# Attention and two gated layers on one core: the planner's order replaced by a written sequence, and the last block's end by product pairs

## The chip, the cores and the metric

The kernel runs on 1 core of a Trainium2 chip. The metric is device time in microseconds (us), the median of a few runs. TensorE (PE) multiplies, VectorE (DVE), ScalarE (ACT) and GpSimd (POOL) work element by element, and SyncE (SP) issues nearly all DMAs. Each engine works through its own queue in order.

## The reference

```python
def _attn_ref(q, k, v, tau):                    # batch 4, heads 8, sequence 576, head size 64
    scores = np.matmul(q, k.transpose(0, 1, 3, 2)) / np.sqrt(64)
    thresh = np.max(scores, axis=-1, keepdims=True) - tau
    scores = np.where(scores >= thresh, scores, -1e9)
    attn = np.exp(scores - np.max(scores, axis=-1, keepdims=True))
    attn = attn / (np.sum(attn, axis=-1, keepdims=True) + 1e-09)
    return np.matmul(attn, v)

x = attn_out.transpose(0, 2, 1, 3).reshape(2304, 512)
h = x @ w_in                                     # 512 x 2048
x = (h * np.tanh(softplus(h))) @ w_out           # 2048 x 512
h = x @ w2_in                                    # 512 x 2048
out = (h * np.clip(h + 3.0, 0.0, 6.0) / 6.0) @ w2_out
```

## The kernel before

**Attention.** The queries of a batch are cut into five tiles of 128 rows (the fifth, the tail, has 64), and two heads go together: 16 head pairs, 80 tiles. Pairs run batch by batch. One tile is a chain of steps: the scores `s` on PE (L1845), their row maximum `pk` on DVE (L1854), the exponentials `ex` on ACT (L1864) with the threshold `th` (L1859), the mask `mk` on DVE (L1867, it reads the scores and writes e_ex), the f16 half `ph` on ACT (L1872) and the rest `pl` on POOL (L730), a DMA transpose `tr` issued by SP (L1880), the product with v, `pv`, on PE (L1893), the division on DVE (L1963 to L1970), a transpose on PE (L2007) and x in two f16 halves. A score tile occupies its PSUM bank until the mask has read it. Loads of attention are `lq` (q, L1760), `lk` (k, L1757; ACT scales k, L1765) and `lv` (v, L1727, with maxima `vm` on DVE, L1709).

**Weights.** The four matrices come as words of 64 bits, in pieces of 1 MB (`lr`, L872). A piece is read by DVE for its top (L786), converted on ACT, POOL and DVE (L938 reads the raw buffer last) and split in f16 halves. There are two raw buffers.

**Layers.** The 2304 tokens are nine blocks of 256: blocks 0 to 7 are two full query tiles of one batch each, block 8 is the four tails. The first product of the first layer (`g`, L1237) of blocks 0 to 5 is worked off in small pieces beside attention. The second product (`y`, L1352) follows. The second layer (L1377 onward) computes both its products from quarters, with seven products in place of eight. For a block there are two units of first-half products (`g0a` to `g1g`, L1426), sums on DVE (L1454, L1519, L1082, L730) and ACT (L1513), the gated halves `oh` on ACT (L1529) and `o` on DVE (L730), then eight feature steps `y` (L1579) of 21 matmuls each, 3 for each of the seven products 0 to 6. The seven sums lie in PSUM, two to a bank. From them the result is put together: ACT takes product 0 as the seed `v` (L1619), DVE adds the others (`va` to `vg`, L1623), and SP stores (L1636).

**What sets the order.** Each step is a task with the engines that may do it, a cost, what it depends on and the buffers it needs. Class `Plan` (L511) keeps a clock for each engine and picks the task that can start next, by priorities, offsets and a table of some thousand corrections (`NUDGE`). Instructions are issued in the order in which tasks are picked. Which buffer of a ring a task takes follows from the order too.

**The last block.** In block 8 the last two feature steps are done pair by pair, in the order `ORDER_OUT`: products 0 and 5, then 6 and 4, then 2 and 3, then 1. The first four lie in one tile of two banks (ring `r_y`, called y_y), the same ring that block 7's sums use, the others in two tiles of one bank each (ring `r_h`). Each quarter of the result is stored by two DMAs of 64 x 256, all on SP's queue, since the tail rows of a pair of batches go to two places.

Of the kernel before, what the change touches and what calls it, by code (L numbers as in the profile page):

```python
# [21 lines left out]
P = 128  # L22
# [15 lines left out]
COL = 4  # L38
ORDER = (0, 0, 0, 0, 1, 0, 0, 1, 1, 1, 1)
LAST = (1, 1)  # L40
ORDER_OUT = (0, 5, 6, 4, 2, 3, 1)
# [3 lines left out]
WARM_WINDOW = 3.413  # L45
RELEASE = dict.fromkeys(("s", "m", "h", "y", "aux"), 0.27)

STEP = 2.791
START = 12
PV_OFF = 3.422  # L50
V_FIRST = -0.435
FIRST_AHEAD = 3
PREP_AHEAD = 5.76
CONV_STEP = 1
CONV_AT = 5.423
LATE_STEP = 3.76
# [24 lines left out]
LAG = 4
# [2141 lines left out]
```

## Time and profile before

| | |
|---|---|
| median of 3 runs | 978.81 us (976.41 to 979.07) |
| span of the profiled execution | 977.3 us |
| PE busy | 923.8 us, 95% |
| DVE busy | 766.2 us, 78% |
| ACT busy | 649.9 us, 66% |
| POOL busy | 401.6 us, 41% |

The profile is one execution, taken by the hardware. Its own time is the span, and the runs' median stands 1.5 us above it. Rows of the timeline give a start, a duration, the engine, the line, the operation, what is written from what, how many instructions are merged in the row, and in brackets the idle time of that engine before it with the instruction that ended it.

### The profile page before, as it was taken

What the parts mean: (1) busy time and instruction counts of PE and PEld (TensorE: products, weight loads), DVE (VectorE), ACT (ScalarE), POOL (GpSimd) and SP (SyncE); (2) the same over time, 40 slices, a digit from 0 to 9 for tenths busy, and PEclk for the clock granted to TensorE, in tenths of its full rate; (3) what the DMA queues carried; (4) which work ended last, traced back from release to release, by engine and by line L of the source; (5) the groups of instructions that cost most, each with busy time, mean ns of one, the idle gap of its engine ahead of it and who ended that gap; (6) DMA issues with size and microseconds to landing.
All of it is one profiled execution on the core that took longest, in us unless ns stands there. A gap on an engine that the chain in (4) does not pass through costs nothing.

```text
span 977.3 us, 25801 instructions
## 1 busy us (share of the span) xinstructions
PE 923.8 (95%) x10776; PEld 799.4 (82%) x10776; DVE 766.2 (78%) x1432; ACT 649.9 (66%) x1051; POOL 401.6 (41%) x354
## 2 busy tenths in 40 slices
PE   3679789999999999999999999999999999999996
PEld 1457467777777778888888888999999999999986
DVE  6987698888888887369999889787767757758864
ACT  6778688888888877567876778565354444444541
POOL 2777676766655666225656777710000000000000
PEclk9759789999999999999999999999999999999999
DMA  9899999999999999864665757760210210110001
GB/s 313 192 238 229 252 227 214 235 258 220 229 224 274 212 218 244 236 245 174 238 218 196 276 185 270 249 223 2 60 61 2 60 57 6 61 40 23 23 17 29
DMA packets 201796, 164.46 MB, mean 168 GB/s; under 512 B 174160, under 2 KB 174928, under 8 KB 195280
## 3 DMA queue, kind: packets, MB, share of 16 engines
q1 hardware_dynamic: 201680, 162.82, 62.0%
q8 instruction: 85, 1.39, 0.6%
q14 instruction: 31, 0.25, 0.1%
HBM read 84.28 MB, written 36.04 MB: 123 GB/s over the span
## 4 chain that ended last, share of the span: by engine, by line
PE 81%; DVE 10%; DMA 5%; ACT 1%; issue 1%; SPq 1%; POOL 1%; DVEq 0%; ACTq 0%; POOLq 0%
PE y_y L1352 16%; PE h_g L1237 16%; PE s_s L1845 8%; PE aux_pv L1893 6%; PE hp_g1a L1426 5%; PE h_g0a L1426 5%; PE hp_g1d L1426 2%; PE h_g0d L1426 2%; DMA raw_lr<-in_moe_w_in 2%; DVE e_ex L1867 2%; DVE nm_pk L1854 1%; DMA pt_tr<-p_ph 1%; PE h_g1b L1426 1%; PE hp_g0b L1426 1%; DVE top L786 1%; PE y_y__1_8_0_14998 L1579 1%
## 5 line engine op out<-in xcount | busy, mean ns | idle before, releaser
L730 POOL TENSOR_TENSOR p_ph<-e_ex,p_ph 128x128 f16<-128x128 f32 (+3 forms) x160 | 185.8, 1184 | 110.7 <-issue 54.8
L1579 PEld LDWEIGHTS <-gs_h 128*128 128x128 f16 x1512 | 146.8, 98 | 18.0 <-issue 1.5
L1426 PEld LDWEIGHTS <-w__h 128*128 128x128 f16 x2016 | 156.0, 98 | 0.6
L1854 DVE TENSOR_REDUCE nm_pk<-s_s 128x1 f32<-128x576 f32 x144 | 104.6, 751 | 31.1 <-PE s_s L1845 30.1
L1867 DVE SCALAR_TENSOR_TENSOR e_ex<-s_s,thr_th,e_ex 128x576 f32<-128x576 f32 x144 | 111.8, 811 | 17.8 <-ACT thr_th L1859 13.2
L1864 ACT ACTIVATE e_ex<-s_s,nm_pk 128x576 f32<-128x576 f32 x144 | 104.1, 730 | 17.0 <-DVE nm_pk L1854 14.2
L1845 PE MATMUL s_s<-kd_lk,qs_qp 64*128 64x288 f32 x440 | 81.7, 487 | 34.0 <-DVE e_ex L1867 25.4
L1872 ACT ACTIVATE p_ph<-e_ex 128x576 f16<-128x576 f32 x144 | 94.8, 679 | 12.5 <-DVE e_ex L1867 8.7
L1426 PEld LDWEIGHTS <-w__u 128*128 128x128 f16 x1008 | 98.6, 98 | 0.0
L1893 PEld LDWEIGHTS <-pt_tr 128*128 128x128 f16 x2016 | 81.8, 103 | 9.9 <-issue 5.8
L1845 PEld LDWEIGHTS s_s<-kd_lk,qs_qp 64*128 64x128 f32 x440 | 42.6, 209 | 55.2 <-issue 35.9
L1893 PE MATMUL aux_pv<-vh,pt_tr 128*128 128x65 f16 (+1 forms) x1296 | 86.6, 204 | 0.8 <-DMA pt_tr<-p_ph 0.8
L730 DVE TENSOR_TENSOR gs_h<-g_ab,gs_h 128x896 f16<-128x896 f32 x72 | 74.6, 1086 | 15.9 <-ACT gs_h L1529 15.9
L1529 ACT ACTIVATE gs_h<-g_ab 128x1792 f16<-128x1792 f32 x36 | 59.6, 1690 | 27.4 <-DVE g_ab L730 27.4
L1893 PE MATMUL aux_pv<-vl_vl,pt_tr 128*128 128x64 f16 x720 | 70.9, 203 | 0.0
L1513 ACT ACTIVATE g_ab<-g_ab,aux,hscales 128x512 f32<-128x512 f32 x72 | 54.1, 805 | 16.9 <-DVE g_ab L1454 16.9
L1286 ACT ACTIVATE he_t<-h_g,hin 128x512 f32<-128x512 f32 x63 | 42.9, 683 | 22.4 <-PE h_g L1237 18.3
L1323 ACT ACTIVATE hp_e<-hl_l 128x512 f32<-128x512 f32 x72 | 42.4, 595 | 21.7 <-DVE gs_h L1332 21.3
L1519 DVE SCALAR_TENSOR_TENSOR g_ab<-g_ab,f 128x512 f32<-128x512 f32 x72 | 51.2, 746 | 5.0 <-ACT g_ab L1513 5.0
L1332 DVE SCALAR_TENSOR_TENSOR gs_h<-hp_e,fscales,gs_h 128x512 f16<-128x512 f32 x72 | 52.9, 742 | 1.9 <-ACT gs_h L1326 1.8
L1326 ACT ACTIVATE gs_h<-hp_e,fscales 128x512 f16<-128x512 f32 x72 | 47.4, 680 | 9.5 <-PE y_y L1352 8.9
L1444 ACT ACTIVATE s_ka<-h_g0a 128x512 f32<-128x512 f32 x27 | 16.1, 595 | 48.4 <-PE h_g0a L1426 48.2
(651 smaller groups left out, 2523.3 us busy)
## 6 DMA issues: line engine op xcount, KB each, us to landing
hd<-he_t SPq DMA_DIRECT2D x36, 512.0 KB, 3.7
hl_l<-hd SPq DMA_DIRECT2D x18, 1024.0 KB, 5.6
raw_lr<-in_moe_w_in SPq DMA_DIRECT2D x16, 1024.0 KB, 5.8
raw_lr<-in_moe_w_out SPq DMA_DIRECT2D x16, 1024.0 KB, 7.4
yd<-yl_zhy SPq DMA_DIRECT2D x9, 896.0 KB, 3.8
qs_qp<-in_q SPq DMA_DIRECT2D x10, 576.0 KB, 6.0
v_lv<-in_v SPq DMA_DIRECT2D x16, 320.0 KB, 4.8
kd_lk<-in_k SPq DMA_DIRECT2D x15, 288.0 KB, 4.2
```

The costliest lines, as they stand in the source:

```text
L730: engine[e].tensor_tensor(dst, a, b, ALU.subtract)
L1237: mm(hv[:, j, :], wj[:, wl, c * P : (c + 1) * P], x.tile[:, c, xl, :], start=j == 0 and n == 0, stop=j == 1 and n == 11, skip_group_check= ...
L1352: mm(yv[:, h, :], wt[1][f // 2].tile[:, f % 2, wl, c * P : (c + 1) * P], gs[fp // COL].tile[:, fp % COL, gl, f % 2, :], start=fp == 0 and ...
L1426: mm(dst.tile[:, i * Q : (i + 1) * Q], wt[2][fp][wl].tile[:, right - 1, c * P : (c + 1) * P], x[xl].tile[:, c, left - 1], start=first and ...
L1529: nc.scalar.activation(part.tile[:, :, 0], g.tile[:, :, 1:], AF.Copy)
L1579: mm(region(p), part[:, gl, left - 1], wt[3][fp][wl].tile[:, right - 1], start=fp == n == 0 and spot(p)[1] == 0, stop=fp == NG - 1 and n == 2,
L1845: mm(s[j].tile[:, half, :HALF], lh[r], rh[r], start=m == 0, stop=m == len(terms) - 1,)
L1854: nc.vector.tensor_reduce(neg.tile[:, j : j + 1], sv(j), AX.XY, ALU.max, negate=True)
L1864: nc.scalar.activation(ev(j), sv(j), AF.Exp, bias=neg.tile[:, j : j + 1])
L1867: nc.vector.scalar_tensor_tensor(ev(j), sv(j), thr.tile[:, j : j + 1], ev(j), ALU.is_ge, ALU.mult)
L1872: nc.scalar.activation(p16.tile[:, js, :S], e_.tile[:, js], AF.Copy)
L1893: mm(ov[:, dst, :d], pt.tile[:, j, ch, :], part.tile[:, src, vc, :], start=i == j == ch == 0 and part is vh, stop=j == w - 1 and ch == 8, ...
```

## The change

The planner's cost model is removed: its constants, `NUDGE`, costs and priorities of all tasks, and the clocks. `Plan.run` now takes the next name from a string of 4094 tokens, each a step and its engine, and issues it. The tasks are the same but for the last block's end, and each runs on the engine that it had, but for one store. The sequence differs from the planner's order locally; on PE it is nearly the same, and the number of PE's instructions is equal.

```diff
-ORDER_OUT = (0, 5, 6, 4, 2, 3, 1)
+ENDS = ((0, 1), (5, 6), (4, 2), (3,))
+END_FPS = 3
...
     def run(self, until=None):
-        while self.left and (until is None or any(t.end is None for t in until)):
-            best = None
-            for e in self.clock:
-                c = self._candidate(e)
...
+        while self.tasks if until is None else not all(t.done for t in until):
+            name, _, e = next(self.sequence).partition("@")
+            task = self.tasks.pop(name)
+            e = e or task.engines[0]
...
         if final:
-            ys = [Buf(r_y), Buf(r_h), Buf(r_h)]
+            ys = [Buf(r) for r in (r_h, r_h, r_hp, r_hp)]
+            spots = {p: ((ys[n], 0), i) for n, ps in enumerate(ENDS) for i, p in enumerate(ps)}
...
-        for fp in range(NG - 2 if final else NG):
-            a = gemm2((fp,), ORDER_OUT if final else range(7))
+        for fp in range(NG - END_FPS if final else NG):
+            a = gemm2((fp,), sum(ENDS, ()) if final else range(7))
             ready = dict.fromkeys(range(7), a)
         if final:
-            for n in range(0, 7, 2):
-                ps = ORDER_OUT[n : n + 2]
-                ready.update(dict.fromkeys(ps, gemm2((NG - 2, NG - 1), ps)))
+            for ps in ENDS:
+                ready.update(dict.fromkeys(ps, gemm2(range(NG - END_FPS, NG), ps)))
...
-        side_, yo = Buf(r_out), Buf(r_out)
+        side_, yo = Buf(r_out), Buf(r_s2 if final else r_out)
...
+        def store_tails(e_, j, half, deps, tag):
+            cols_ = slice(half * BLK, (half + 1) * BLK)
+            rows = out.rearrange("(b s) n -> b s n", b=B)[2 * j : 2 * j + 2, FULL:, cols_]
+
+            def go(e):
+                queue = nc.sync if e == "sp" else nc.scalar
+                queue.dma_start(out=rows, in_=yo.tile[:, j, cols_])
...
         if final:
+            c11 = step(lambda: result(1, 1), 1, lambda: temp(0), [s1], "g")
+            store_tails("sp", 1, 1, [c11], "st3")
+            u2 = step(lambda: temp(1), 5, lambda: temp(0), [s1], "a")
+            u3 = step(lambda: temp(2), 6, lambda: temp(1), [u2], "b")
+            c22 = step(lambda: result(0, 0), 4, lambda: temp(2), [u3], "c")
+            store_tails("sp", 0, 0, [c22], "st0")
+            v = step(lambda: temp(3), 2, lambda: temp(1), [u2], "e")
+            c12 = step(lambda: result(1, 0), 4, lambda: temp(3), [v], "f")
+            store_tails("sp", 1, 0, [c12], "st1")
+            c21 = step(lambda: result(0, 1), 3, lambda: temp(2), [u3], "d")
+            store_tails("act", 0, 1, [c21], "st2")
```

**Three places of the order.** The first is DVE at its first two tiles, behind the constants. L1854 (L1701 in the changed kernel) is the row maximum of one head's scores, L1709 (L1587) a maximum of a part of v, L1867 (L1714) the mask. Before:

```order
L1854 TENSOR_REDUCE nm_pk_0_0_1_195<-s_s_0_0_0_184 128x1
L1709 TENSOR_REDUCE vt_vm_0_1_199<-v_lv_0_0_173 128x1
L1709 TENSOR_REDUCE vt_vm_0_1_199<-v_lv_0_0_175 128x1
L1709 TENSOR_REDUCE vt_vm_0_1_199<-v_lv_0_0_177 128x1
L1854 TENSOR_REDUCE nm_pk_0_0_1_195<-s_s_0_1_0_191 128x1
L1709 TENSOR_REDUCE vt_vm_0_1_199<-v_lv_0_0_180 128x1
L1867 SCALAR_TENSOR_TENSOR e_ex_0_0_2_201<-s_s_0_0_0_184,thr_th_0_0_1_212,e_ex_0_0_2_201 128x576
L1867 SCALAR_TENSOR_TENSOR e_ex_0_0_2_201<-s_s_0_1_0_191,thr_th_0_0_1_212,e_ex_0_0_2_201 128x576
```

and in the changed kernel:

```order
L1701 TENSOR_REDUCE nm_pk_0_0_1_194<-s_s_0_0_0_189 128x1
L1701 TENSOR_REDUCE nm_pk_0_0_1_194<-s_s_0_1_0_179 128x1
L1587 TENSOR_REDUCE vt_vm_0_1_199<-v_lv_0_0_170 128x1
L1587 TENSOR_REDUCE vt_vm_0_1_199<-v_lv_0_0_166 128x1
L1714 SCALAR_TENSOR_TENSOR e_ex_0_0_2_197<-s_s_0_0_0_189,thr_th_0_0_1_201,e_ex_0_0_2_197 128x576
L1714 SCALAR_TENSOR_TENSOR e_ex_0_0_2_197<-s_s_0_1_0_179,thr_th_0_0_1_201,e_ex_0_0_2_197 128x576
L1587 TENSOR_REDUCE vt_vm_0_1_199<-v_lv_0_0_175 128x1
L1587 TENSOR_REDUCE vt_vm_0_1_199<-v_lv_0_0_172 128x1
```

The second head's row maximum moved ahead of the maxima of v, two of which moved behind the masks.

The second place is SP around the load of the eighth weight piece of the first matrix (`raw_lr_7`). `pt_tr` is a tile's transpose, `kd_lk` and `qs_lq` are k and q of a head pair, `hd` a store of the first layer's h. Before:

```order
L1880 DMA_TRANSPOSE pt_tr_2_1_1_1278<-p_ph_2_1_1_1182 128x18x128
L1757 DMA kd_lk_6_0_1317<-in_k 128x576
L1294 DMA hd_104<-he_t_0_0_1_1161 128x1024
L1760 DMA qs_lq_6_0_1345<-in_q 128x2x576
L1880 DMA_TRANSPOSE pt_tr_3_1_1_1347<-p_ph_3_1_1_1272 128x18x128
L872 DMA raw_lr_7_0_1382<-in_moe_w_in 128x1024
L1880 DMA_TRANSPOSE pt_tr_4_0_1_1387<-p_ph_4_0_1_1343 128x9x128
```

and in the changed kernel:

```order
L1626 DMA kd_lk_6_0_1271<-in_k 128x576
L1727 DMA_TRANSPOSE pt_tr_2_0_1_1282<-p_ph_2_0_1_1128 128x18x128
L1167 DMA hd_104<-he_t_0_0_1_1152 128x1024
L758 DMA raw_lr_7_0_1348<-in_moe_w_in 128x1024
L1727 DMA_TRANSPOSE pt_tr_3_0_1_1350<-p_ph_3_1_1_1266 128x18x128
L1629 DMA qs_lq_6_0_1409<-in_q 128x2x576
L1727 DMA_TRANSPOSE pt_tr_4_0_1_1413<-p_ph_4_0_1_1306 128x9x128
```

The weight load moved ahead of the transpose of the fourth tile, and q of the seventh pair behind it. The third, fourth and seventh weight loads stand one transpose earlier in the same way, k of the fourth pair and q of the sixth and eighth later.

The third place is the end of DVE's queue, the additions of the last block (L1623, L1491 in the changed kernel). `y_y_0__1_8_0` is the tile of two banks, `h_y` and `hp_y` are tiles of one. Before:

```order
L1623 SCALAR_TENSOR_TENSOR out_v_8_1_15175<-y_y_0__1_8_0_14998,xscale,out_v_8_1_15175 128x256 x2
L1623 SCALAR_TENSOR_TENSOR out_va_8_2_15177<-y_y_0__1_8_0_14998,xscale,out_v_8_1_15175 128x256
L1623 SCALAR_TENSOR_TENSOR out_v_8_1_15175<-h_y_0__1_8_1_14999,xscale,out_v_8_1_15175 128x256
L1623 SCALAR_TENSOR_TENSOR out_va_8_2_15177<-h_y_0__1_8_1_14999,xscale,out_v_8_1_15175 128x256
L1623 SCALAR_TENSOR_TENSOR out_va_8_2_15177<-y_y_0__1_8_0_14998,xscale,out_v_8_1_15175 128x256
L1623 SCALAR_TENSOR_TENSOR out_va_8_2_15177<-h_y_0__1_8_2_15000,xscale,out_v_8_1_15175 128x256
```

and in the changed kernel:

```order
L1491 SCALAR_TENSOR_TENSOR out_v_8_1_15167<-h_y_0__1_8_1_14993,xscale,out_v_8_1_15167 128x256
L1491 SCALAR_TENSOR_TENSOR s_va_8_2_15187<-h_y_0__1_8_0_14992,xscale,out_v_8_1_15167 128x256
L1491 SCALAR_TENSOR_TENSOR out_v_8_1_15167<-h_y_0__1_8_1_14993,xscale,out_v_8_1_15167 128x256
L1491 SCALAR_TENSOR_TENSOR s_va_8_2_15187<-hp_y_0__1_8_2_14994,xscale,out_v_8_1_15167 128x256
L1491 SCALAR_TENSOR_TENSOR out_v_8_1_15167<-hp_y_0__1_8_2_14994,xscale,out_v_8_1_15167 128x256
L1491 SCALAR_TENSOR_TENSOR s_va_8_2_15187<-hp_y_0__1_8_2_14994,xscale,out_v_8_1_15167 128x256
L1491 SCALAR_TENSOR_TENSOR s_va_8_2_15187<-hp_y_0__1_8_3_14995,xscale,out_v_8_1_15167 128x256
```

The additions now follow the pairs, each pair in its own bank, and the last one alone reads the fourth tile (product 3). On PE two feature steps of block 7 moved from ahead of the last two first-half products of block 8 to behind them, so that they stand directly before the last block's first step; and six of block 7's additions stand on DVE among the gated halves of block 8 in place of ahead of them.

## Rows read from the trace of the kernel before

**Rows 1.** The page: busy time of PE; PE's granted clock in 40 slices.

```profile
PE 923.8 (95%) x10776; PEld 799.4 (82%) x10776; DVE 766.2 (78%) x1432; ACT 649.9 (66%) x1051; POOL 401.6 (41%) x354
...
PEclk9759789999999999999999999999999999999999
```

**Rows 2.** Busy time of engines by stretches: start:end, length, busy, clock, DMA share, GB/s.

```profile
0.00:74.00 74.00, 43.14 (x370) 29.20 (x371) 61.42 (x116) 51.92 (x89) 44.10 (x54) 0.78 0.91 247
74.00:100.00 26.00, 25.73 (x282) 20.49 (x282) 20.55 (x48) 22.52 (x42) 19.80 (x21) 0.97 0.96 229
100.00:120.00 20.00, 13.51 (x113) 8.62 (x114) 13.03 (x30) 12.75 (x23) 11.22 (x13) 0.75 1.07 246
120.00:137.00 17.00, 12.67 (x133) 9.06 (x132) 14.55 (x34) 14.71 (x27) 12.13 (x11) 0.80 1.11 237
137.00:950.00 813.00, 810.26 (x9716) 715.63 (x9712) 642.65 (x1180) 541.29 (x867) 314.32 (x259) 1.00 0.59 160
950.00:977.00 27.00, 18.50 (x168) 16.37 (x168) 13.96 (x27) 6.69 (x7) 0.00 (x0) 0.93 0.13 40
```

**Rows 3.** Timeline of PE before 137 us: scores, with the idle time ahead.

```profile
13.08 2.29 PE L1845 MATMUL s_s<-kd_lk,qs_qp 64*128 64x288 f32 x8 [5.18 <-DVE e_ex L1867]
...
38.50 1.24 PE L1845 MATMUL s_s<-kd_lk,qs_qp 64*128 64x288 f32 x8
...
103.87 1.33 PE L1845 MATMUL s_s<-kd_lk,qs_qp 64*128 64x288 f32 x4 [3.94 <-DVE e_ex L1867]
...
128.82 0.76 PE L1845 MATMUL s_s<-kd_lk,qs_lq 64*128 64x288 f32 x4 [2.94 <-issue]
```

**Rows 4.** Timeline of DVE before 137 us: waits for loads.

```profile
8.32 2.50 DVE L1709 TENSOR_REDUCE vt_vm<-v_lv 128x1 f32<-128x640 f32 x3 [1.09 <-DMA v_lv<-in_v]
10.73 0.75 DVE L1854 TENSOR_REDUCE nm_pk<-s_s 128x1 f32<-128x576 f32 x1
...
44.82 1.22 DVE L786 TENSOR_REDUCE top<-raw_lr 128x1 f32<-128x1024 f32 x1 [0.84 <-DMA raw_lr<-in_moe_w_in]
...
57.76 1.22 DVE L786 TENSOR_REDUCE top<-raw_lr 128x1 f32<-128x1024 f32 x1 [1.52 <-DMA raw_lr<-in_moe_w_in]
...
100.69 1.22 DVE L938 SCALAR_TENSOR_TENSOR cvt_c__1_1258<-raw_lr,cvt_c__1_1258 128x1024 uint32<-128x1024 uint32 x1
...
112.32 1.22 DVE L786 TENSOR_REDUCE top<-raw_lr 128x1 f32<-128x1024 f32 x1 [2.96 <-DMA raw_lr<-in_moe_w_in]
```

**Rows 5.** Timeline of SP's queue: transposes, and the eighth weight load behind one.

```profile
32.29 6.61 SPq L1880 DMA_TRANSPOSE pt_tr<-p_ph  x2
...
100.22 6.01 SPq L1880 DMA_TRANSPOSE pt_tr<-p_ph  x1
106.32 0.53 SPq L872 DMA_DIRECT2D raw_lr<-in_moe_w_in  x1
```

**Rows 6.** DMA issues: count, size of one, median us from issue to landing.

```profile
kd_lk<-in_k SPq DMA_DIRECT2D x15, 288.0 KB, 4.2
...
out<-out_va SPq DMA_DIRECT2D x8, 64.0 KB, 2.0
```

**Rows 7.** Timelines of PE, DVE, ACT and SP at the end.

```profile
951.17 0.27 PE L1579 MATMUL y_y__1_8_0_14998<-w__h,gs_h 128*128 128x256 f16 x1 [1.33 <-DVE out_va L1623]
...
968.86 0.82 PE L1579 MATMUL h_y__1_8_2_15000<-w__wl,gs_h 128*128 128x256 f16 x6
...
949.88 0.76 DVE L1454 TENSOR_TENSOR g_ab<-hp_g1d,s_ka 128x256 f32<-128x256 f32 x2 [0.56 <-PE hp_g1d L1426]
...
957.91 4.10 DVE L730 TENSOR_TENSOR gs_h<-g_ab,gs_h 128x896 f16<-128x896 f32 x4 [1.03 <-ACT gs_h L1529]
...
970.87 0.48 DVE L1623 SCALAR_TENSOR_TENSOR out_va<-h_y__1_8_2_15000,xscale,out_v 128x256 f32<-128x256 f32 x1
...
967.75 0.47 ACT L1619 ACTIVATE out_v<-y_y__1_8_0_14998,xscale 128x256 f32<-128x256 f32 x1 [8.29 <-PE y_y__1_8_0_14998 L1579]
...
969.80 5.02 SPq L1636 DMA_DIRECT2D out<-out_va  x8
```

More of the change, by code (lines that the diff above doesn't have):

```diff
@@ L483, in __init__ @@
     def __init__(self, ring):
-        self.ring, self.slot, self.left, self.end, self.tile = ring, None, 0, 0.0, None
+        self.ring, self.slot, self.left, self.last, self.tile = ring, None, 0, 0, None
         ring.unclaimed += 1
@@ L497, in drop @@
             _, n, make, i = self.slot
-            self.ring.free.append((self.end, n, make, i))
+            self.ring.free.append((self.last, n, make, i))
             self.ring.settle()
 class Task:
-    def __init__(self, engines, fn, deps, bufs, prio, off, dma, name):
-        self.engines, self.fn, self.bufs = engines, fn, bufs
-        self.prio, self.off, self.dma, self.name = prio, off, dma, name
-        self.waiting, self.after, self.ready = 0, [], {}
-        self.deps, self.end, self.engine = deps, None, None
-        self.kind = name.rstrip("0123456789_")
@@ L537, in add @@
+class Plan:
+    def __init__(self):
+        self.tasks, self.at = {}, 0
+        self.sequence = iter(SEQUENCE.split())
+    def add(self, engines, fn, deps=(), bufs=(), name="", order=()):
+        after = [d for d in (*deps, *order) if d is not None]
+        task = Task(engines, fn, after, list(bufs), name)
         for b in task.bufs:
             b.left += 1
-        for d in (*task.deps, *order):
-            if d is not None and d.end is None:
-                task.waiting += 1
-                d.after.append(task)
@@ L543, in add @@
-        self.left += 1
-        if task.waiting == 0:
-            self._release(task)
-        return task
-    def _release(self, task):
-        for e in task.engines:
-            t = 0.0
-            for d in task.deps:
-                t = max(t, d.end + self.LATENCY.get((d.engine, e), 0.15))
-            if e == "pe":
-                t += PAD.get(task.kind, 0.0)
-            task.ready[e] = t
-            self.open[e].append(task)
-        if task.prio is None:
-            task.prio = max(min(task.ready.values()), min(self.clock.values())) + task.off
@@ L632, in run @@
[L632 to L647 removed]
+        assert name not in self.tasks, name
@@ L648, in run @@
+        self.tasks[name] = task
+        return task
+    def run(self, until=None):
+        while self.tasks if until is None else not all(t.done for t in until):
+            name, _, e = next(self.sequence).partition("@")
+            task = self.tasks.pop(name)
+            e = e or task.engines[0]
+            assert e in task.engines and all(d.done for d in task.after), name
             for i, b in enumerate(task.bufs):
                 if b.slot is None:
-                    b.take(f"{b.ring.name}_{task.name}_{i}")
@@ L651, in run @@
-            task.engine = e
-            if e == "dve" and len(task.engines) > 1:
-                start = max(start - self.slow, self.clock[e])
-            cost = task.engines[e]
-            if e == "pool" and self.give:
-                cost += YIELD
-            if e == "pe":
-                if (task.kind == "s") != self.halves:
-                    cost += HALVES[self.halves]
-                    self.halves = not self.halves
-                cost = self._clocked(start, cost, 0.75 if task.kind == "s" else 1.0)
@@ L662, in run @@
-            end = start + cost
-            self.clock[e] = end
-            if e == "dve" and task.kind in PORT:
-                self.port = end
-            if e == "sp":
-                self.dma = max(self.dma, end + 1.1) + task.dma
-                if task.kind == "tr":
-                    self.clock[e] = max(end, self.dma - 0.95)
-                end = self.dma + 1.1
-            task.end = end
+                    b.take(f"{b.ring.name}_{name}_{i}")
+            self.at += 1
             task.fn(e)
-            if e == "pool" and self.give:
-                self.give()
+            task.done = True
@@ L675, in run @@
             for b in task.bufs:
-                b.drop(end)
-            self.left -= 1
-            for n in task.after:
-                n.waiting -= 1
-                if n.waiting == 0:
-                    self._release(n)
+                b.drop(self.at)
 @with_exitstack
@@ L730, in sub @@
         engine[e].tensor_tensor(dst, a, b, ALU.subtract)
-    def pick(which, **cost):
-        return {e: cost[e] for e in WHO[which]}
     NG = NF // 2
@@ L1703, in batch_values @@
         col = xinv[:, b : b + 1]
[L1705 to L1706 removed]
+        task = named(f"{b}")
         def v_max(e, i, vb):
@@ L1930, in query_tiles @@
-            parts = []
-            for js in whole(MERGE_LO):
-                size = (js.stop - js.start) * S
-                cost = {"dve": 0.17 + size / 960.0, "pool": 0.1 + size / 450.0}
-                parts.append(
-                    go(
-                        {x: cost[x] for x in P_LO}, lambda e, js=js: p_lo(e, js),
-                        [phs[j] for j in heads[js]], [e_, p16], "pl", js.stop - 1,
-                    )
-                )
-            a = go({"sp": 0.7}, transpose, parts, [p16, pt], "tr", w - 1, TR_DMA * w, 0.0, [prev[2]])
@@ L1952, in normalise @@
+            return go(("pe",), pv, [a, before, split], [pt, o, vh, vl], "pv")
+        def normalise(cs, o, last):
             den = Buf(r_den)
@@ L2098, in fused_kernel @@
     r_st = [ring(f"st{i}", None, 0, None) for i in range(2)]
-    now = plan.clock["dve"]
-    plan.slow, plan.near = SLOW_LATE, NEAR_LATE
     factor_tasks()
```

1046 lines of the change are left out of this document (612 added, 434 removed), and 323 rows, old and new, of the table NUDGE.

## The prediction

> **What bounds the kernel now.** I read the page's first two parts, then PE's busy time stretch by stretch, then the idle time in front of single instructions. On the page [rows 1] the reader is to see that PE is busy for 923.8 of the 977.3 us of the span, and that its granted clock is below full speed only in the first five or six of forty slices. The table by stretches [rows 2] says where the other 53 us are: 30.9 before 74 us (74.00 less 43.14), 0.3 from 74 to 100, 6.5 from 100 to 120, 4.3 from 120 to 137, 2.7 in the 813 us from 137 to 950, and 8.8 after 950. So from 137 us on PE is the bound, with nothing between its instructions. The change leaves PE's matmuls as they are (as many, of the same sizes, mostly in the same order), so only three things can move the end: the idle time and half-clock time before 137 us, the few stalls, and the end. A microsecond that PE wins before 137 us is a microsecond off the end as long as PE stays full behind it.
>
> The head has two causes. Up to 74 us nothing but attention can run on PE, since the first block's x is not complete before; DVE is busy for 61.4 of 74 us there, and PE's gaps mostly end on the mask (the line of e_ex) on DVE [rows 2, 3]. So the head's length is DVE's sum plus DVE's own waits. From 74 to 137 us there is first-layer work, but twice PE stands before a score: 3.94 us at 103.87 and 2.94 us at 128.82 [rows 3].
>
> **The end, part one: the stall before the last block.** At 951.17 us PE starts the last block's products after 1.33 us of idle, released by DVE's reads of the accumulator of block 7 [rows 7]. In the new order two feature steps of block 7 stand between the last first-half product and the last block's first step. A step is 21 matmuls; the last block's 168 take 18.50 us [rows 2], 0.110 each, so a step is 2.3 us and two are 4.6. The last block starts in single banks, which the first-half products have left by then, not in the accumulator that block 7 has just left. The 1.33 us go: **-1.3**. What is late next are the gated features: DVE finished the last of them at 962.01 (957.91 and 4.10), 12.1 us after the last first-half product, which releases it at 949.88 [rows 7], and has six additions of block 7 (0.4 us each) and their waits in front of it in the new order, so 15 to 16 us; PE wants it after two steps of block 7 and five of block 8, 7 x 2.3 = 16. That is tight: I price it at 0, and keep 1.5 us of stall for the range.
>
> **The end, part two: the tail.** The last matmul ends at 969.68 us (968.86 and 0.82), and the span 7.6 us later [rows 7]. In these 7.6 us the reader sees DVE reading until 971.35 and SP issuing eight stores one behind the other for 5.02 us, from 969.80 to 974.8. The seed on ACT had waited 8.29 us for the accumulator's tile, which holds two banks with products 0, 5, 6 and 4 and is complete only with the third pair. Now each pair has a tile, the final three features are done pair by pair, and only product 3 (9 matmuls, 1.0 us) comes last; its only reader is one addition. After the last matmul stand then: one addition 0.48 us, one issue 5.02/8 = 0.63, and what lay behind the last issue in the profile, 977.3 less 974.8 = 2.5. The new stores carry twice as much each; the 288 KB load lands in 4.2 us and the 64 KB store in 2.0 [rows 6], so 128 KB by the same line takes 2.6: +0.6. Sum 4.2 to 4.3 in place of 7.6: **-3.3**. Bounds: -2.0, if the three stores on SP's queue still hold up the fourth or the landing is 4.2, and -4.0 if the size costs nothing. Here the trace has no store issued by ACT; I take SP's issue.
>
> **The head to 74 us.** The reader sees on DVE [rows 4] three maxima of v (0.8 each, after 1.09 us of waiting for v's load) in front of the second half of the very first row maximum, which so comes at 10.73 us; the score behind it waits 5.18 us [rows 3]. Now both row maxima stand first. DVE also stands 0.84 and 1.52 us before the top of a weight load, at 44.82 and 57.76. These loads go out behind transposes on SP's queue, which waits for the split on POOL at each; in the new order each stands one transpose earlier. The three waits are 1.09 + 0.84 + 1.52 = 3.45 us of a chain that DVE bounds. I take **-3.0**; bounds 0, if others grow, and -5, if the first score comes 2 us earlier besides.
>
> **74 to 137 us.** SP spends 6.01 us at one transpose at 100.22 and only then issues the eighth weight load, at 106.32 [rows 5], though DVE's last read of the buffer that it goes to ends at 101.91 (100.69 and 1.22, [rows 4]). DVE waits for that load until 112.32, idle 2.96 us [rows 4], with row maxima, masks and so scores queued behind it. In the new order the load stands ahead of its transpose. It could go 4.4 us sooner, and DVE's 2.96 us vanish. PE's idle time from 74 to 137 us is 11.1 us in all [rows 2]; I take half of it, **-5.4**, since the gap at 128.82 has another releaser. PE's 26.2 busy us from 100 to 137 ran at a clock of 0.75 and 0.80, which is 13.51 x 0.25 + 12.67 x 0.20 = 5.9 us of lost clock; a third comes back with the shorter gaps: **-2.0**. Bounds for both: 0 and -14.
>
> **What the order may break.** A changed order of some 4000 steps brings waits that no row of before can show. I charge one gap of the size of those seen, 2.94 to 3.94 us [rows 3]: **+3.0**, bounds 0 and +8 (two).
>
> **Sum.** -1.3 - 3.3 - 3.0 - 5.4 - 2.0 + 3.0 = -12.0. The profiled span is 977.3 us, and the median of the runs, 978.81, lies 1.5 above it. So a span of 965.3, and a median of about 967. The planner's removal itself costs nothing on the chip: it runs while the program is built.
>
> **Rivals.** *Only the end counts* (B). In the head the DMA engines are full: a share of 0.91, 0.96, 1.07 and 1.11 in the four stretches [rows 2]. A load issued earlier then takes from the transposes beside it what it wins. For it: transposes and loads share the stretch in which PE waits. Against it: the share is as high from 100 to 137 as to 100, where PE loses 0.3 us in 26. Then -1.3 - 3.3 = -4.6, and the time is 974. The Trainium skill says the like (DMA: Bandwidth & Descriptors, "Issuing engines are not separate DMA queues"): whoever issues them, DMAs run on the same 16 engines and interleave, and another issuer saves only the time of issuing. By it the fourth store on ACT's queue gains no more than an issue.
>
> *The head is mended* (C). All of the 11.1 us and most of the lost clock between 74 and 137 go, since the scores' gaps and the low clock feed each other: -4.6 - 3.0 - 11 - 4 = -22, 957 us. For it: full clock and no gap from 137 us on, with the same kinds of work. Against it: some gaps there end on PE's own issue.
>
> *Slower through SP's queue* (D). Four loads of attention go behind a transpose where they stood ahead of it: k of the fourth head pair and q of the sixth, seventh and eighth. A transpose stands on SP until POOL's split is done; the pair of them at 32.29 ends at 38.9 [rows 5]. The fourth pair's k would be issued behind the first of these, at about 35.6, land 4.2 us later [rows 6] and be scaled on ACT; its score stood at 38.50 [rows 3] and would start at about 41: 2.5 us late, with DVE, the bound, idle meanwhile. If all four loads cost that and the head wins nothing, the sum is 4 x 2.5 - 4.6 = +5.4, 984 us. It decides from three such waits on with the head's gain lost. Against it: the later pairs are loaded a whole pair ahead.
>
> *The order hardly matters* (E): the head loses by one such wait or two what the end wins, -4.6 + 4 = about 0: 978.
>
> **How the numbers follow.** Differences under 0.3% (2.9 us) can't be told from none here. Forecast around 967 (962 to 971): 0.42. B, 971 to 976: 0.25. C, under 962: 0.13. E, within 2.9 us: 0.11. D, slower: 0.09. Faster is the first three, 0.80; same 0.11; slower 0.09. The range leaves out D, most of E and the end of C: 955 to 977.
>
> **What would show it.** In the changed kernel's trace: no idle time before the last block's first matmul, and some 4.3 us from the last matmul to the end, with four stores; a first row maximum's second half before 9 us, no wait of DVE for a weight load over 1 us before 137, the eighth load issued before its transpose; PE's idle time from 74 to 137 near 6 us and a clock there above 0.8. It would be wrong if PE waits for scores in stretches where it was full (137 to 400 above all), if a score waits for k or q, or if the last block's late features hold PE for more than 1.5 us.

## The result: slower by 1.1%, and the profile after

The changed kernel takes 990.12 us (median of 4, 988.28 to 992.9) where the one before takes 978.94 beside it (976.41 to 981.0): a ratio of 1.0113, 95% interval 1.009 to 1.0136. The forecast was 967, range 955 to 977: 12 us faster, where 11 us slower came out. The profiled execution has a span of 986.5 us, 9.2 above the one of before.

First the stretches, to be read beside [rows 2] (same columns; the clock is the third number from the end, the DMA share the one behind it):

```profile
0.00:74.00 74.00, 41.69 (x359) 27.73 (x360) 57.17 (x112) 48.64 (x82) 41.10 (x50) 0.79 0.91 234
74.00:100.00 26.00, 25.08 (x266) 18.87 (x265) 23.78 (x50) 22.92 (x45) 23.29 (x21) 0.94 1.07 242
100.00:120.00 20.00, 14.72 (x156) 9.92 (x154) 16.74 (x35) 16.11 (x27) 13.70 (x14) 0.91 1.12 258
120.00:137.00 17.00, 13.19 (x160) 9.31 (x157) 16.28 (x34) 13.40 (x27) 11.82 (x13) 1.00 1.02 232
...
137.00:250.00 113.00, 108.64 (x1303) 85.43 (x1300) 93.11 (x168) 93.60 (x174) 71.79 (x68) 0.98 1.06 232
250.00:400.00 150.00, 146.76 (x1782) 116.51 (x1780) 118.55 (x216) 117.07 (x222) 91.96 (x86) 1.00 1.07 225
400.00:950.00 550.00, 549.09 (x6550) 508.63 (x6549) 423.43 (x787) 325.70 (x469) 143.95 (x108) 1.00 0.37 129
...
972.00:977.00 5.00, 1.78 (x17) 1.35 (x14) 1.97 (x5) 0.00 (x0) 0.00 (x0) 1.00 0.10 29
977.00:982.00 5.00, 0.00 (x0) 0.00 (x0) 0.00 (x0) 0.00 (x0) 0.00 (x0) 0.60 0.13 44
982.00:986.40 4.40, 0.00 (x0) 0.00 (x0) 0.00 (x0) 0.00 (x0) 0.00 (x0) 0.50 0.10 36
```

Then two longer stretches, first before, then after (in these tables a matmul that straddles a border counts on both sides, so starts are read from one long stretch):

```profile
0.00:137.00 137.00, 95.06 (x894) 67.37 (x896) 109.55 (x227) 101.91 (x178) 87.25 (x96) 0.81 0.97 242
137.00:400.00 263.00, 260.94 (x3196) 206.07 (x3193) 215.15 (x390) 215.44 (x401) 167.39 (x156) 1.00 1.07 231
```

```profile
0.00:137.00 137.00, 94.69 (x930) 65.83 (x931) 113.97 (x228) 101.07 (x178) 89.92 (x95) 0.86 0.98 239
137.00:400.00 263.00, 255.40 (x3082) 201.94 (x3079) 211.66 (x383) 210.67 (x395) 163.75 (x153) 0.99 1.06 228
```

The reader is to see three things. Up to 137 us PE is idle for 42.3 us (32.3 and 0.9, 5.3, 3.8), as before (42.0), but the clock from 100 to 137 is 0.91 and 1.00 in place of 0.75 and 0.80; 930 matmuls of PE have started by then, 894 before. From 137 to 400 us it is idle for 7.6 us, before for 2.1. And from 977 us nothing computes any more, yet there are 9.5 us to come, with a DMA share of 0.13: two engines of sixteen.

The end of the queues of PE, DVE, SP and ACT, beside [rows 7], with the issues' view (size, median us to landing) and the page's row of ACT's DMA queue:

```profile
972.64 1.15 PE L1448 MATMUL hp_y__1_8_3_14995<-w__wl,gs_oh 128*128 128x256 f16 x9
...
974.15 0.47 DVE L1491 SCALAR_TENSOR_TENSOR s_va<-hp_y__1_8_3_14995,xscale,out_v 128x256 f32<-128x256 f32 x1
...
971.85 2.93 SPq L1505 DMA_DIRECT2D out<-s_va  x3
...
974.66 1.14 ACTq L1505 DMA_DIRECT2D out<-s_va  x1
...
out<-s_va SPq DMA_DIRECT2D x3, 128.0 KB
out<-s_va ACTq DMA_DIRECT2D x1, 128.0 KB
...
q10 hardware_dynamic: 130, 0.13, 0.0%
```

One addition and one issue stand behind the last matmul, as forecast, and the last issue ends at 975.80. The span goes on for 10.7 us. ACT's queue has 130 records: 128 rows of 1 KB and two short ones.

Then the waits of PE from 137 to 410 us (in total, times, longest), of after and, below, of before:

```profile
PE aux_pv L1740 <- DMA pt_tr<-p_ph: 5.1, 7, 2.2
PE s_s L1692 <- DVE den_dt L1775: 1.2, 1, 1.2
...
PE s_s L1692 <- DMA qs_lq<-in_q: 0.4, 1, 0.4
```

```profile
PE aux_pv L1893 <- DMA pt_tr<-p_ph: 0.8, 2, 0.6
PE aux_fl L2007 <- DVE xn_dn L1970: 0.8, 1, 0.8
PE s_s L1845 <- DVE e_ex L1867: 0.3, 1, 0.3
```

In the changed kernel PE waits seven times for a tile's transpose, before only twice and shortly.

### The profile page after: what moved, and what is told of

The parts are those of the page before. It is cut to its first block, busy times and chain, and to the rows that moved or that the text cites. A ratio compares the mean times of both kernels' runs of the same rounds, so it can differ in the third digit from the quotient of the medians.

```text
span 986.5 us, 25747 instructions
## 1 busy us (share of the span) xinstructions
PE 923.0 (94%) x10776; PEld 797.5 (81%) x10776; DVE 768.1 (78%) x1432; ACT 646.3 (66%) x1051; POOL 397.6 (40%) x354
## 4 chain that ended last, share of the span: by engine, by line
PE 65%; DVE 12%; DMA 8%; ACT 6%; POOL 5%; issue 2%; SPq 2%; DVEq 0%; ACTq 0%; POOLq 0%
PE h_g L1111 12%; PE y_y L1225 10%; DMA pt_tr<-p_ph 5%; PE s_s L1692 5%; PE hp_g1a L1298 5%; PE h_g0a L1298 5%; PE aux_pv L1740 4%; PE h_g0d L1298 2%; PE hp_g1d L1298 2%; DVE nm_pk L1701 2%; POOL p_ph L626 2%; DVE e_ex L1714 2%; SPq L1727 1%; PE h_g1b L1298 1%; PE hp_g0b L1298 1%
## 5 line engine op out<-in xcount | busy, mean ns | idle before, releaser
L1448 PEld LDWEIGHTS <-gs_oh 128*128 128x128 f16 x1512 | 146.1, 98 | 16.4
L1714 DVE SCALAR_TENSOR_TENSOR e_ex<-s_s,thr_th,e_ex 128x576 f32<-128x576 f32 x144 | 113.3, 812 | 32.9 <-ACT thr_th L1706 24.6
L1692 PE MATMUL s_s<-kd_lk,qs_lq 64*128 64x288 f32 x560 | 100.1, 474 | 27.7 <-DVE e_ex L1714 15.3
L1701 DVE TENSOR_REDUCE nm_pk<-s_s 128x1 f32<-128x576 f32 x144 | 104.6, 751 | 27.1 <-PE s_s L1692 26.3
L626 DVE TENSOR_TENSOR gs_oh<-g_ab,gs_oh 128x896 f16<-128x896 f32 x72 | 77.1, 1085 | 25.7 <-ACT gs_oh L1398 25.7
L1692 PEld LDWEIGHTS s_s<-kd_lk,qs_lq 64*128 64x128 f32 x560 | 52.7, 204 | 54.5 <-issue 35.0
L1398 ACT ACTIVATE gs_oh<-g_ab 128x1792 f16<-128x1792 f32 x36 | 60.9, 1694 | 38.6 <-DVE g_ab L626 23.5
L1205 DVE SCALAR_TENSOR_TENSOR gs_gh<-hp_e,fscales,gs_gh 128x512 f16<-128x512 f32 x72 | 53.0, 743 | 16.3 <-ACT gs_gh L1199 16.2
L1199 ACT ACTIVATE gs_gh<-hp_e,fscales 128x512 f16<-128x512 f32 x72 | 48.3, 681 | 3.4 <-PE y_y L1225 1.6
L680 DVE TENSOR_REDUCE top<-raw_lr 128x1 f32<-128x1024 f32 x32 | 38.7, 1209 | 0.9 <-DMA raw_lr<-in_moe_w_in 0.9
```

What stands on the lines that cost most here:

```text
L626: engine[e].tensor_tensor(dst, a, b, ALU.subtract)
L1398: nc.scalar.activation(part.tile[:, :, 0], g.tile[:, :, 1:], AF.Copy)
L1448: mm(region(p), part[:, gl, left - 1], wt[3][fp][wl].tile[:, right - 1], start=fp == n == 0 and spot(p)[1] == 0, stop=fp == NG - 1 and n == 2,
L1692: mm(s[j].tile[:, half, :HALF], lh[r], rh[r], start=m == 0, stop=m == len(terms) - 1,)
L1701: nc.vector.tensor_reduce(neg.tile[:, j : j + 1], sv(j), AX.XY, ALU.max, negate=True)
L1714: nc.vector.scalar_tensor_tensor(ev(j), sv(j), thr.tile[:, j : j + 1], ev(j), ALU.is_ge, ALU.mult)
```

## Experiments

All ratios are to the kernel before, run beside each kernel. `stores16` in the diffs stands for the first experiment's edit; all later kernels have it. "New" is the changed kernel's order, "old" the one of before; `old(...)` takes the same steps in the old order. The steps of both orders carry the same names, so parts can be joined.

| run | order | stores of the last block | median us | ratio (95%) |
|---|---|---|---|---|
| the change | new | four of 2 x 64 x 256 | 990.12 | 1.0113 (1.009 to 1.0136) |
| e1 | new | eight of 64 x 256 | 982.19 | 1.0032 (1.0016 to 1.0048) |
| e14 (e1 again) | new | eight | 981.96 | 1.0021 (1.0004 to 1.0038) |
| e2 | old up to the last block's end | eight | 973.64 | 0.9942 (0.9923 to 0.9961) |
| e13 (e2 again) | old up to the last block's end | eight | 973.76 | 0.9950 (0.9935 to 0.9966) |
| e3 | new to 137 us, then old | eight | 984.23 | 1.0053 (1.0032 to 1.0074) |
| e9 | new to 130 us, then old | eight | 982.82 | 1.0036 (1.0021 to 1.0051) |
| e10 | old to 130 us, then new | eight | 981.44 | 1.0035 (1.0019 to 1.0052) |
| e11 | old to 253 us, then new | eight | 982.86 | 1.0037 (1.0021 to 1.0053) |
| e4 | new, ACT's ph moved | eight | 1002.21 | 1.0239 (1.0215 to 1.0263) |
| e5 | new, PE's order old | eight | 1111.35 | 1.1363 (1.1345 to 1.1381) |
| e6 | new, ACT's order old | eight | 1211.22 | 1.2371 (1.2337 to 1.2405) |
| e7 | new, DVE's order old | eight | 1172.34 | 1.1993 (1.1971 to 1.2014) |
| e8 | new, SP's order old | eight | 1076.41 | 1.1003 (1.0977 to 1.103) |
| e12 | new, PE filled at seven waits | eight | 979.98 | 1.0 (0.9983 to 1.0018) |

**e1: the stores on sixteen engines.**

```diff
-                queue.dma_start(out=rows, in_=yo.tile[:, j, cols_])
+                for b in range(2):
+                    queue.dma_start(out=rows[b], in_=yo.tile[b * TAIL : (b + 1) * TAIL, j, cols_])
```

> The changed kernel with one thing altered: each quarter of the last block is stored by two transfers of 64 x 256, as before the change, on the same queues (three quarters on SP, the last on ACT). Theory 'two engines': the four 2 x 64 x 256 stores ran on two of the sixteen DMA engines (130 records of ACT's queue, a DMA share of 0.13 in the last 12 us), and that alone made the tail 13 us. Then the tail after the last matmul falls to 4.5 to 5.5 us, the span from 986.5 to about 978, the median to about 981. Rival 'cold queue': the store on ACT's queue is late because it is the first transfer there (2.6 us from the end of its issue to its first packet). Then the last quarter still ends some 9 us after the last matmul, and the span is 981 or more.

982.19 us: 8 us off. Its repetition e14 has the clearer tail; the last matmuls, the last store's issue, the issues' view, the row of ACT's DMA queue and the stretch behind the last matmul:

```profile
975.34 1.15 PE L1440 MATMUL hp_y__1_8_3_14995<-w__wl,gs_oh 128*128 128x256 f16 x9
...
977.36 1.37 ACTq L1499 DMA_DIRECT2D out<-s_va  x2
...
out<-s_va SPq DMA_DIRECT2D x6, 64.0 KB, 2.0
out<-s_va ACTq DMA_DIRECT2D x2, 64.0 KB, 2.3
...
q10 hardware_dynamic: 160, 0.13, 0.1%
...
977.00:981.30 4.30, 0.00 (x0) 0.00 (x0) 0.32 (x1) 0.00 (x0) 0.00 (x0) 1.00 0.37 92
```

From the last matmul's end (976.49) to the end of the span (981.3) it is 4.8 us, in the changed kernel 12.7 (973.79 to 986.5). The 7.9 us between them are the 8 us between the medians. The last quarter still goes out on ACT's queue and lands in 2.2 to 2.3 us, so the rival, a late first transfer there, falls. What was late was the form of the transfer: two rows of a batch pair outermost, and with them two engines. The edit also makes eight transfers of four, each of half the size; the records tell which of these counts. In the changed kernel ACT's one store left 128 rows and 2 short records, here its two stores left 128 rows and 32. That fits one short record for each engine of a transfer, two engines there and sixteen here, and the DMA share behind the last matmul, 0.13 and 0.37, goes with it.

**e2: the old order with the new end.**

```diff
-SEQUENCE = new
+SEQUENCE = old(steps of new ahead of block 7's fourth feature step) + new(from there on), stores16
```

> The new code and the new end (16-engine stores), but all steps ahead of block 7's fourth feature step stand in the order of the kernel before. Theory: the time lost ahead of the end is lost by the order alone. Then the last matmul starts near 968 us (969.4 before, less the 1.33 us stall), the tail is 5 us: span 973, median 974.5. Rival 'other code': rings and buffers taken in another way cost time by themselves; then it stays within 2 us of the first kernel of this batch (978).

973.64 us, as expected, and 973.76 again in e13: faster than both kernels. So the new end as it was meant is worth 5 us (4.6 was forecast), and the new order alone costs 8.2 us (e14 less e13, on one chip: 981.96 less 973.76). The rival, that the new code costs by its rings, falls.

**Where in the order: e3, e9, e10, e11.**

```diff
-SEQUENCE = new
+SEQUENCE = new[:657] + old(rest) + new end      # e3
+SEQUENCE = new[:633] + old(rest) + new end      # e9
+SEQUENCE = old[:633] + new(rest)                # e10
+SEQUENCE = old[:1433] + new(rest)               # e11
```

> The new order up to the product with v of the first tile of the second batch (about 137 us), then the order of before up to block 7's fourth feature step, then the new end with 16-engine stores. Theory: the new order wins 4 us by 137 us (PE's 900th matmul stands at 133.7 in place of 138.0) and loses 8 us from there to 410; with the middle of before the 4 us are kept: span 969, median 970.5, 4 us under the second kernel. Rival 'debt': the lead at 137 us is borrowed from ACT and DVE work put off, and is paid back whatever the middle's order; then it is within 1 us of the second kernel.

984.23 us, slower than e2 by 10.6. PE stands 8.44 us before a score at 149.85, just behind the cut, where the two orders had not begun the same steps. That is a seam of my making, and the run tells little of either order. The next three cut where the orders have begun all but four to six of the same steps.

> New end with 16-engine stores in all three of this batch. The new order for its first 633 steps (to about 130 us), then the order of before; the cut lies where the two orders have started all but six of the same steps, so no seam as in the third experiment. Beside the second experiment (order of before throughout, 973.6 us). Theory 'middle': PE's lost time at 137 us is the same under both orders (40.0 and 40.8 us), and the 8.6 us are lost from 137 to 410; then 972 to 975. Rival 'head': the new head leaves work put off that is paid later: 979 to 982.

982.82 us, against theory "middle". One gap stands behind the cut, at the transpose of a tail on PE, which waits for ACT; and ACT had stood before the scaling of k:

```profile
138.16 0.77 ACT L1630 ACTIVATE kd_lk<-kd_lk,qscale 128x576 f32<-128x576 f32 x1 [5.63 <-DMA kd_lk<-in_k]
...
142.74 0.48 PE L1821 MATMUL aux_fl<-istack,xtail 128*128 128x64 f32 x1 [4.45 <-ACT xtail L1790]
```

The new order does not have this wait there, and ACT's 5.63 us say where it comes from: a seam again. Among the six steps that differ at the cut are the load of k of the eighth pair and its scaling on ACT. They stand 45 places apart in the new sequence and 56 in the old; behind the cut it is three, so ACT stands until the load has landed. Apart from this gap PE is idle for 1.9 us from 137 to 400 us (6.3 less 4.45), as in the old order. So the trace speaks for theory "middle" and not for "head". The time does not show it: the profile is of an execution of 980.13 us, and what the median has above that no profile shows.

> The order of before for the first 633 steps, then the new order. Theory 'middle': all of the loss is here: 980 to 983, with PE idle some 7 to 8 us between 137 and 400 us. Rival 'head': 973 to 976.

981.44 us: with the head of before, the new order from 130 us costs what the whole new order costs (981.96). This is as theory "middle" had it. Idle time of PE from 137 to 400 us is 7.6 us here, as in the changed kernel.

> The order of before for the first 1433 steps (to about 253 us), then the new order. By the idle time of the first experiment's trace, 4.9 of the 8.5 us between 137 and 400 lie before 250 us and 3.7 behind: under 'middle' 976 to 979, under 'head' 973 to 976.

982.86 us, 4 to 7 above what was expected. Here too a gap of 3.06 us stands behind the cut, before a score at 258.02, and the rest of the waits are those of the new order behind 253 us. The gap is the same kind of seam: a load of v and its maximum on DVE, 80 places apart in the new sequence and 26 in the old, stand side by side behind the cut.

```profile
256.33 0.82 DVE L1582 TENSOR_REDUCE vt_vm<-v_lv 128x1 f32<-128x640 f32 x1 [4.19 <-DMA v_lv<-in_v]
```

So three of the four cuts brought a gap of 3 to 8 us of their own. Behind the cut of e10 no load stands among the steps that differ, and its trace has no such gap; it is the one that can be read.

The stretches of e13 (old order, the first block) and e14 (new order, the second) side by side:

```profile
0.00:137.00 137.00, 93.86 (x894) 65.82 (x896) 109.55 (x227) 101.79 (x178) 87.19 (x96) 0.83 0.94 238
74.00:137.00 63.00, 51.93 (x525) 38.53 (x525) 48.16 (x111) 49.75 (x90) 42.92 (x43) 0.85 0.96 225
137.00:250.00 113.00, 111.19 (x1345) 87.01 (x1344) 94.06 (x169) 94.76 (x174) 74.02 (x69) 0.99 1.06 236
250.00:400.00 150.00, 149.89 (x1852) 119.01 (x1849) 121.07 (x221) 120.95 (x228) 93.40 (x87) 1.00 1.07 229
```

```profile
0.00:137.00 137.00, 94.09 (x926) 65.53 (x927) 113.65 (x228) 100.88 (x177) 89.88 (x94) 0.86 1.00 237
74.00:137.00 63.00, 52.00 (x585) 38.20 (x583) 56.95 (x117) 53.06 (x97) 49.47 (x45) 0.98 1.10 241
137.00:250.00 113.00, 108.61 (x1307) 85.57 (x1304) 93.13 (x169) 93.72 (x174) 71.95 (x68) 0.98 1.04 234
250.00:400.00 150.00, 144.65 (x1763) 114.49 (x1761) 117.39 (x211) 116.24 (x220) 89.77 (x83) 1.00 1.07 224
```

From 74 to 137 us PE starts 60 matmuls more under the new order, with the same idle time and a higher clock; but it was behind at 74 us, and over the whole 137 us it is 32 more (926 against 894). From 137 to 250 us it starts 38 fewer, and from 250 to 400 us 89 fewer, with 4.4 and 5.4 us of idle time against 1.8 and 0.1. The lead is more than given back. PE's busy time in the whole span is nearly the same (922.4 us under the new order, 923.1 under the old), so the 7.9 us between the two spans (981.3 and 973.4) are idle time, and 7.8 of them lie from 137 to 400 us (9.7 against 1.9). In the trace of e1, the same kernel as e14, the clock from 74 to 137 us was 0.87 and the lead small, and the time the same.

**Which engine: e4 to e8.** In the traces it took some 1.9 us (137 to 250 us) and 4.1 us (250 to 410) on average from a tile's last mask to the end of its last half `ph` on ACT under the new order, 0.9 and 1.4 under the old: of 64 full tiles, ACT has exponentials of another tile or h of the first layer between the two halves in 23 cases, in the old order in 6. And PE came to the product with v 3.8 to 4.0 us after the end of the transpose's issue in three traces of the new order, 4.7 us in three of the old (medians). That gave two theories, ACT late or PE early.

```diff
-... mk4_4_0@dve ... ex5_2_0@act ... th5_2_0@act ex5_2_1@act ... ph4_4_0@act
+... mk4_4_0@dve ph4_4_0@act ... ex5_2_0@act ... th5_2_0@act ex5_2_1@act ...      # e4, 73 such moves
```

> The changed kernel with 16-engine stores; besides, from the fourth pair's tail tile on, ACT's f16 half of each head's weights (ph) stands directly behind its mask (73 steps moved). Theory 'ACT order': in the changed kernel ACT does exponentials of the next tile or h of the first layer between the two halves of a tile, so the second half starts 2.1 to 3.7 us after the mask (0.9 to 1.4 before), the transpose is late, and PE waits for it in 137 to 410 us. Then PE's gaps ahead of pv fall from 5 us to under 2, and the time is 3 to 5 us under the first kernel: span 974. Rival 'wrong place': the halves put first push the exponentials back, scores wait for their bank, and the sum is the same or worse: 978 or more.

1002.21 us. PE's waits from 137 to 410 us:

```profile
PE s_s L1687 <- DVE e_ex L1709: 9.6, 12, 1.4
PE h_g L1104 <- ACT he_t L1152: 4.4, 2, 3.1
...
PE aux_pv L1735 <- DMA pt_tr<-p_ph: 0.9, 1, 0.9
```

The waits for transposes did go, from 6.8 us in e14 to 0.9. In their place scores wait for their bank, which the mask frees. That the mask comes later because ACT does the exponentials later is what the rival had said; the trace agrees with it but does not prove it. The rival had this mechanism but not its size.

Then one engine at a time was put back into its old order, the others kept (in a few places, where the two orders can't be joined, a step moved by one):

```diff
-SEQUENCE = new
+SEQUENCE = new, steps of one engine in their old order among themselves      # e5 PE, e6 ACT, e7 DVE, e8 SP
```

> The new order with 16-engine stores (first experiment, 982.2 us), but PE works in its order of before; the other engines keep the new order. Theory 'PE too early': in the new order PE reaches the product with v 0.8 us sooner after the transpose's issue (3.95 in place of 4.79 us, median), and that costs the waits for transposes, some 5 of the 8.6 us between the orders. Then the time falls by 4 to 6, to about 977. Rival 'ACT late': the f16 half waits on ACT behind the next tile's exponentials, and PE's place only shows it; then it stays within 2 us of 982.

> The same with ACT alone in its order of before. Theory 'PE too early': within 2 us of 982, since PE comes as early as in the new order. Rival 'ACT late': the two halves stand together again, the chain from score to transpose is 1.4 us shorter, and the waits for transposes go: 976 to 978.

> The same with DVE alone in its order of before. By both theories DVE's order is not what costs: within 2 us of 982. A third, 'DVE': DVE bounds the head, and its new order (two row maxima first) is 2.5 us worse by 74 us; then 979 or less.

> The same with SP alone in its order of before. Theory 'loads behind transposes' (rival D of the prediction): k of the fourth pair and q of the sixth to eighth come late in the new order; with SP's order of before the waits of scores for k and q go (1.8 us at the fourth pair, 0.7 at 247 us), but weight loads stand behind transposes again: 979 to 980. By the two others: within 2 us of 982.

1111, 1211, 1172 and 1076 us: all far slower, where changes of at most 6 us were expected. None tells which engine's order costs the 8 us. They show something else. The old order of PE differs from the new one by 1.4 places on average, that of SP by 2.0, ACT 2.3 and DVE 3.3, each order is good with its own partners, and one engine out of step costs 10 to 24%. One thing isn't separated in this: which buffer of a ring a step takes follows the joint sequence, and joining moved that too. In e7, over the whole span, the scores alone waited for masks 34 times:

```profile
PE s_s L1687 <- DVE e_ex L1709: 74.3, 34, 13.5
```

**e12: are the waits for transposes plain loss?**

```diff
-pv4_2_0@pe pk5_2_1@dve ex5_2_0@act g60_6_0_1@pe c1_0_l@dve g60_8_0_1@pe th5_2_0@act g60_10_0_1@pe
+g60_6_0_1@pe g60_8_0_1@pe g60_10_0_1@pe pv4_2_0@pe pk5_2_1@dve ex5_2_0@act c1_0_l@dve th5_2_0@act
```

and the like, with two or three pieces, at six more tiles.

> The first experiment (new order, 16-engine stores) with PE's order altered at seven places, those at which its trace shows PE waiting for a transpose from 137 to 410 us: two or three pieces of the first layer's product that stood behind the product with v stand ahead of it. Theory 'plain loss': the seven waits (4.7 us in the first experiment's trace) go and nothing follows: 3 to 5 us under e14. Rival 'chain': the tiles are late, DVE and ACT get their next work later, other gaps take their place: within 1.5 us of e14, or slower.

979.98 us, 2.0 under e14, between the two theories; the intervals of the two ratios overlap a little. PE's waits for transposes from 137 to 410 us, e14 above, e12 below:

```profile
PE aux_pv L1734 <- DMA pt_tr<-p_ph: 6.8, 6, 2.2
```

```profile
PE aux_pv L1734 <- DMA pt_tr<-p_ph: 4.1, 4, 1.7
```

In these two profiles 2.7 us of waiting went, and 2.0 us of the median; but e1, the same kernel as e14, has 4.7 us of such waits, so the fall is not that certain. At the seven tiles that were filled the waits fell from 5.6 us (4.7 in e1) to 1.8, at two others they grew from 1.2 to 2.3. What could be filled looks like plain loss for the most part. The rest of the 8 us was not reached: two of the waits stayed though work was put ahead of them.

> The second experiment's kernel again, beside the others on one chip: 972 to 975 if what it showed holds.

> The first experiment's kernel again, beside the others on one chip: 980 to 984.

Both came as expected (in the table).

## Why the prediction was wrong, step by step

**The stall before the last block: right.** Forecast -1.3. In the changed kernel and in e13 no idle time stands before the last block's first matmul, and the late features, which I had called tight, held nothing up.

**The tail: the mechanism right, the price wrong, and that is 8 of the 23 us between forecast and result.** Forecast 4.2 to 4.3 us from the last matmul to the end; e13 and e14, with stores of the old form, have 4.7 and 4.8 (e13: 968.67 to 973.4). The changed kernel has 12.7, 5.1 more than before. The failed step is "128 KB by the same line takes 2.6": I priced the new stores by their size, from two rows [rows 6], and bounded the landing at 4.2. Both rows were of transfers with 64 or more rows outermost. The new form has two outermost, and its four transfers shared two engines: their records lie between 973.1 and 985.3 us, 12.2 us for the four, where I had let each land in 2.6. The Trainium skill (DMA: Bandwidth & Descriptors, "Why a DMA increments its semaphore by 16 and not by 1") states the rule: a DMA runs on the largest number of engines up to 16 that divides the slowest dimension of both sides, here 2 and 128, so two. The share of 0.13 agrees. I had weighed another section of that page and not this one.

**The head to 74 us: wrong.** Forecast -3.0. The three waits did shrink: DVE's idle time for weight loads is 0.9 us in the whole changed kernel (page, below), where [rows 4] alone have 5.3. But PE's idle time to 74 us went from 30.9 to 32.3, and DVE's own from 12.6 to 16.8 (74.00 less 61.42 and 57.17).

```profile
L680 DVE TENSOR_REDUCE top<-raw_lr 128x1 f32<-128x1024 f32 x32 | 38.7, 1209 | 0.9 <-DMA raw_lr<-in_moe_w_in 0.9
...
8.37 1.42 DVE L1701 TENSOR_REDUCE nm_pk<-s_s 128x1 f32<-128x576 f32 x2 [3.62 <-PE s_s L1692]
...
41.90 0.82 DVE L1587 TENSOR_REDUCE vt_vm<-v_lv 128x1 f32<-128x640 f32 x1 [1.14 <-DMA v_lv<-in_v]
...
36.11 0.58 SPq L1626 DMA_DIRECT2D kd_lk<-in_k  x1
...
40.31 1.00 PE L1692 MATMUL s_s<-kd_lk,qs_qp 64*128 64x288 f32 x6 [0.57 <-ACT kd_lk L1634]
```

The step that failed is "three waits of a chain that DVE bounds": I took away the waits that I saw and not those that the new order brings. The row maxima end at 9.79 in place of 11.48, but the first score starts at 6.03 in place of 5.10, a new wait of 1.14 us for v's load stands on DVE at 41.90, and rival D's first place came at about the time that it gave: k of the fourth pair goes out behind a transpose, at 36.11 (35.6 was the estimate), and its score starts at 40.31 (41) in place of 38.50. PE's wait for it is 0.57 us.

**74 to 137 us: partly as forecast, and worth nothing in the end.** Forecast -5.4 of idle time and -2.0 of clock. The eighth weight load goes out at 102.83 (106.32 before) and DVE waits 0.93 for it (2.96). PE's idle time is 10.0 us (11.1), and the clock is up here and in e14 (0.95 and 0.98 from 74 to 137 us, 0.85 before), though hardly in e1 (0.87). At 137 us 36 more matmuls have started than before. They are not alike: in the traces products with v start some 0.03 us apart, those of the layers up to 0.11, so the lead is an estimated 1 to 4 us. But e10, without this head, takes as long as e14 with it. The failed step is the sentence that a microsecond won before 137 us is one off the end "as long as PE stays full behind it". The condition was mine, and I did not price its failing.

**What the order may break: +3.0 taken, at most +8 allowed; 5.5 to 7.8 measured.** The waits are in 137 to 400 us, where the rows of before show PE nearly full and I had put no term: PE's idle time there is 7.6 us in the changed kernel against 2.1, and 9.7 in e14 against 1.9 in e13. The term had the right reason and too small a size, and the head's gain that was to outweigh it did not come. I had named "137 to 400 above all" as the place that would prove me wrong. Runs e13 and e14 show that the order, its head included, costs 8.2 us, e10 that the part from 130 us on suffices.

**The rivals.** D was right in sign, and its 984 lies near the 982 of the new order without the fault of the stores, but that is luck. Of the four waits of 2.5 us that it priced the trace shows 0.57 us for k at 40.31 and 0.38 us for q at 244.09. Most of the idle time from 137 to 400 us is waits for transposes (5.1 of 7.6 us); whether PE comes too early or the transposes too late, e4 to e8 do not decide. B's time, "only the end counts", is what e2 gives with the end as meant: 973.6, where I had 974. But e2 has the old head, so B's reason, that transposes lose what an earlier load wins, was not tested. (C's terms add up to -22.6 and 956, not 957; it changes nothing.)

The sum: 978.8 - 5.1 (the end as meant, e13) + 8.2 (the order) + 8.1 (stores on two engines) = 990.0, and 990.1 was measured. This is no proof of its own: the three terms are differences of measured times from one kernel to the next, so they must close. Set against the forecast, the end as meant is 0.5 better, the stores 8.1 worse, and head and order together +8.2 where -3.0 - 5.4 - 2.0 + 3.0 = -7.4 was forecast: 15.6 worse. That is the 23 us.

Open is which steps of the new order cost the 8 us from 130 us on, beyond the 2 that e12 won: it is known that PE stands idle there and mostly for transposes, but no single engine's order can be exchanged to find why.

## What to carry to other kernels

Before a DMA's access pattern is merged into fewer transfers, look at its outermost dimension on both sides: two rows outermost mean two engines, and four stores of 128 KB at the very end then cost 8 us more than eight of 64 KB with 64 rows outermost. An order of steps on in-order engines is one piece: it is judged on the chip as a whole, gains in one stretch may be given back in the next, halves of two orders joined were no faster than the slower of the two (981.4 to 984.2 us), and one engine's order with the others' was far worse (1076 to 1211). Whoever cuts and joins two orders should look whether a load and the step that needs it come to stand side by side at the cut: in three of four cuts here they did, and an engine waited 4 to 6 us for the load. Where a change has several parts, build each alone: here the old order with the new end beats both kernels, at 0.995.

## What the runs showed that I had not expected

- The number of DMA engines follows the shape: a store of 2 x 64 x 256 left 130 records (128 rows and two short ones: two engines), share 0.13; two stores of 64 x 256 left 160 (128 and 32), and each landed in 2.0 to 2.3 us.
- A store on ACT's otherwise unused queue was issued in 1.14 us (1.37 for two), SP's in 0.5 to 0.66 each, and landed in 2.2 to 2.3 us: no penalty that the time shows.
- One engine's queue changed by 1.4 to 3.3 places on average, with the others kept: 10 to 24% slower (1076 to 1211 us).
- The granted clock from 74 to 137 us was 0.87 in one profile and 0.98 in another of the same kernel (e1 and e14), with 8.6 and 11.0 us of idle time and the same time in all (982.19 and 981.96): in these two profiles less idle time went with a lower clock, so neither alone says what a stretch is worth.
